# Threshold attention into a bilinear FFN: one head's keys per partition half, turned weights moved unit by unit

## The chip, the cores and the metric

The kernel runs on one core of a Trainium2 chip. The metric is the time on the device in microseconds, from the start to the end of the program. The times of one kernel on this chip differ from run to run by a few microseconds. All arithmetic is in fp32.

## The reference

Inputs: q, k, v of 8 batches x 8 heads x 576 rows x 64, a scalar tau of 0.02, and three FFN weight matrices of float64 (512 x 1536 twice, 1536 x 512).

```python
scores = scale * np.matmul(q, k.transpose(0, 1, 3, 2))
thresh = np.max(scores, axis=-1, keepdims=True) - tau
scores = np.where(scores >= thresh, scores, -1000000000.0)
scores = scores - np.max(scores, axis=-1, keepdims=True)
attn = np.exp(scores)
attn = attn / (np.sum(attn, axis=-1, keepdims=True) + 1e-09)
attn_out = np.matmul(attn, v)
# (B,H,S,D) -> (B*S, H*D)
x = attn_out.transpose(0, 2, 1, 3).reshape(B * S, H * D)
out = (x @ w_a) * (x @ w_b) @ w_out
```

So each head has a 576 x 576 matrix of weights, of which only the scores near the row's maximum are not zero; its product with v is 64 wide, and the eight heads of a row side by side are one token of 512 for the FFN.

## The kernel before

**Tiles.** Two heads make a pair; there are 32 pairs (`pairs`, four per batch). The rows of a pair are cut into five *units*: u = 0 to 3 are 128 query rows of both heads, u = 4 (`NT`) is the tail, the last 64 rows of both heads in one tile. That makes 160 units, in the order of the list `units`: for each batch first u = 0 and 1 of its four pairs, then u = 2, 3 and 4 of each pair. (Batch 0 has an order of its own: all u = 0, all u = 1, then 2 and 3 of each pair, then the four tails.)

**Slots.** The main loop runs over *slots* g. Slot g computes the scores of unit g (`scores`, matmuls at L337), takes their row maximum on VectorE (L344), the exponential on ScalarE (L372) into a tile `tw`, and the comparison with the threshold together with the row sum on VectorE (L375); the rows are divided by their sum on ScalarE (L394). Slot g+1 turns the weights of unit g, since the product with v needs the keys on the partitions. This is done in two steps: VectorE transposes blocks of 32 x 32 (`turn_blocks`, L445 and L458), and then DMAs carry the blocks to a DRAM buffer `swap` (L453, L465) and back into SBUF in the turned order (`turn_back`, L476). Two units, u = 0 and 1, or u = 2, 3 and the tail, make a *half*: `turn_blocks` writes after the second one, in four DMAs from a tile that both share; the tail adds four. One DMA brings the whole half back into `turned_sb`, of which there is one for halves. `PV_LAG` = 4 slots after the half's last unit the product with v is computed (`weighted`, `product`, L491), with v as the stationary operand and the turned weights moving. The first eight units (`BY_PE`) are turned on TensorE instead (`turn_pe`, L418 and L424), and their product follows two slots later (`weighted_unit`).

**The product.** 1152 keys of two heads lie in nine blocks of 128 partitions: blocks 0 to 3 and half of block 4 belong to head 0, the rest to head 1. A matmul reads 64 partitions (the half r) and writes 64 (the half j, one head). Each head has its keys on both halves, so each head has two sums, one per PSUM bank, and `join` adds them: a copy of the first on ScalarE (L480) and an addition of the second on VectorE (L481). Block 4 is used once by each head, on (r, j) = (0, 0) and (1, 1).

**The FFN.** When all four pairs of a half of a batch are done, their 256 tokens become a block for the FFN (`ffn`, L622, L683, L728, L774), whose matmuls are cut into small steps. `advance` works off steps between the pieces of attention, as many as a pace says: `pace` is worked out from the backlog and the slots left until the next block arrives, and the columns of products with v are set against it (`running["owed"]`).

**Order.** Each engine executes its instructions in the order in which the loop emits them (`keep_order`). SyncE (SP) issues nearly all DMAs, one queue in that order: in a slot first weights for the FFN, then `turn_blocks`' writes, then `turn_back`'s read, then loads of q, k and v, then output stores. A DMA that has to wait holds up those behind it.

**TensorE's quarters.** All large matmuls are 64 x 64: they use one quarter of the 128 x 128 array, chosen by the half of the partitions that they read and the half that they write. An fp32 matmul is recorded as two passes. Scores of a full unit use all four quarters; those of a tail have head 0's result in the upper half and head 1's in the lower, so they use (0, 1) and (1, 0) alone (`o = t if u < NT else 1 - j`).

Of the kernel before, what the change touches and what calls it, by code (L numbers as in the profile page):

```python
# [10 lines left out]
FP32 = mybir.dt.float32  # L11
# [11 lines left out]
PV_LAG = 4  # L23
# [10 lines left out]
RAWS = 4  # L34
BY_HEAD = 16
# [16 lines left out]
def kernel(  # L52
# [81 lines left out]
    def load(i, name, engine=nc.sync):  # L134
# [7 lines left out]
        for j in range(2):  # L142
            rows = src[b, 2 * hp + j].rearrange("(n e) d -> e n d", e=Q)
            for h in range(2):
                r = slice((2 * j + h) * Q, (2 * j + h + 1) * Q)
                engine.dma_start(t[r], rows[:, n0:n1, h * Q:(h + 1) * Q])
# [10 lines left out]
    def load_v(i):  # L157
        b, hp = pairs[i]
        vm = loads.tile([P, NSLOT, D], FP32, tag="vm", bufs=HP, name="vm")
        rows = v[b, 2 * hp:2 * hp + 2].rearrange("j s d -> (j s) d")  # L160
        nc.sync.dma_start(vm, rows.rearrange("(s p) d -> p s d", p=P))
        loaded[i]["v"] = vm
# [36 lines left out]
    turned_sb = const.tile([P, NSLOT * (HALF + TAIL)], FP32, name="turned_sb")  # L199
# [66 lines left out]
    t = work.tile([P, 2 * NB, 2 * Q], FP32, tag="tw", bufs=2, name="rows")  # L266
    t = t.rearrange("p n e -> p (n e)")[0:R]
    rooms = [t[:, c:c + ROWS] for c in range(0, 3 * ROWS, ROWS)]
# [29 lines left out]
    prepared, scored, weights, turned, tbufs = {}, {}, {}, {}, {}  # L298
    x_of, xtail_of = {}, {}
    blocks, complete, swaps, ready = [], [], {}, []  # L300
# [47 lines left out]
    def rooms_of(i, u):  # L348


        g = units.index((i, u))
        if u == NT and i >= HP:
            return [work.tile([P, NB, Q], FP32, tag="wt", bufs=1, name="wt")]
        if (i == 0 if u == NT else g % 2 == 0 if g < BY_PE else u % 2 == 0):
            state["tw"] = work.tile([P, 2 * NB, 2 * Q], FP32, tag="tw", bufs=2, name="tw")
        t = state["tw"]
        if u < NT and g >= BY_PE:
            return [t[:, j * NB:(j + 1) * NB, (u % 2) * Q:(u % 2 + 1) * Q] for j in range(2)]
        t = t.rearrange("p n e -> p (n e)").rearrange("p (z n e) -> p z n e", z=4, e=Q)
        return [t[:, i]] if u == NT else [t[:, g % 2 * 2 + j] for j in range(2)]  # L360
# [44 lines left out]
    def turned_at(c, n):  # L405
        return turned_sb[:, c:c + NSLOT * n].rearrange("p (s w) -> p s w", w=n)

    def turn_pe(i, u):

        ws, dg = weights.pop((i, u))  # L410
        ws = [w.rearrange("p n e -> p (n e)") for w in ws]
        wT = turned_at(units.index((i, u)) % 2 * NSLOT * P, P)
        turned[i, u, "pe"] = wT
        tp = banks(512, "tp").rearrange("p j (s q) -> p j s q", s=NT)
        for j, w in enumerate(ws):
            for s in range(NT):
                c = TAIL * j + s * P
                nc.tensor.matmul(tp[:, j, s, :], w[:, c:c + P], dg[:, j], start=True, stop=True)  # L418
        for j in range(2):
            nc.scalar.copy(wT[:, 5 * j:5 * j + NT], tp[:, j])  # L420
        tp = banks(P, "tp")[:, 0]
        for j, w in enumerate(ws):
            c = MAIN * (1 - j)
            nc.tensor.matmul(tp[TAIL * j:TAIL * (j + 1)], w[:, c:c + TAIL], dg[:, j],  # L424
                             start=True, stop=True)
        nc.vector.tensor_copy(wT[:, NT], tp)
# [10 lines left out]
    def turn_blocks(i, u):  # L437

        ws, _ = weights.pop((i, u))
        if u < NT:  # L440
            if u % 2 == 0:
                tbufs[i] = state["tw"]
            tb = tbufs[i]
            for w in ws:
                nc.vector.transpose(w, w)  # L445
            if u % 2 == 0:
                return
            h = u // 2
            n = width(i, h)
            swap = scratch.tile([2 * NB, Q, n], FP32, tag=f"swap{n}", name="swap")  # L450
            swaps[i, h] = swap
            for g in range(G):
                nc.sync.dma_start(  # L453
                    swap[:, :, g * 2 * Q:(g + 1) * 2 * Q].rearrange("c p w -> p c w"),
                    tb[g * Q:(g + 1) * Q])
        else:
            tb = ws[0]
            nc.vector.transpose(tb, tb)  # L458
            if i < HP:
                swaps[i, 2] = scratch.tile([2 * NB, Q, TAIL], FP32, tag="swapt", name="swap")  # L460
            swap = swaps[part(i, u)]
            for g in range(G):
                c = slice((1 - g // 2) * NB, (2 - g // 2) * NB)
                w0 = swap.shape[2] - TAIL + (g % 2) * Q
                nc.sync.dma_start(swap[c, :, w0:w0 + Q].rearrange("c p w -> p c w"),  # L465
                                  tb[g * Q:(g + 1) * Q])
        if part(i, u):
            ready.append(part(i, u))

    def turn_back(count):  # L470

        for _ in range(count):
            i, h = ready.pop(0)
            n = width(i, h)
            wT = turned_at((i - 1) % HP * NSLOT * TAIL if n < HALF and i else NSLOT * HALF if n < HALF else 0, n)
            nc.sync.dma_start(wT, swaps.pop((i, h)).rearrange("(s r) p w -> (r p) s w", r=G))  # L476
            turned[i, h] = wT
# [5 lines left out]
    def product(wT, vm, n):  # L483

        pv = banks(n, "pv")
        for s in (NT, 0, 1, 2, 3):
            for r in range(2):
                rows = slice(r * D, (r + 1) * D)
                for j in ((r,) if s == NT else range(2)):
                    k0 = NT if s == NT else 5 * j + s  # L490
                    nc.tensor.matmul(pv[j * D:(j + 1) * D, r], vm[rows, k0], wT[rows, k0],  # L491
                                     start=(s == (NT if j == r else 0)), stop=(s == NT - 1))
        return pv

# [24 lines left out]
    def weighted_unit(i, u):  # L519

        b, hp = pairs[i]
        pv = product(turned.pop((i, u, "pe")), loaded[i]["v"], P)
# [3 lines left out]
        join(x_of[b, 0][:, hp, u * P:(u + 1) * P], pv[:, 0], pv[:, 1])  # L526
# [6 lines left out]
    def weighted(i, h):  # L533
# [3 lines left out]
        pv = product(turned.pop((i, h)), loaded[i]["v"], n)  # L537
        if h < 2:
            if hp == 0:
                x_of[b, h] = x_tile("xT")  # L540
            lo, hi = (pv[:, r, 0:HALF].rearrange("p (i t e) -> p i t e", t=2, e=Q) for r in range(2))
            join(x_of[b, h][:, hp, :].rearrange("p (t i e) -> p i t e", t=2, e=Q), lo, hi)
            if hp == HP - 1:
                complete.append((x_of.pop((b, h)), ("half", b, h)))
        if n % HALF:
# [3 lines left out]
            join(xtail_of[b // GT][:, hp, t * TAIL:(t + 1) * TAIL], pv[:, 0, n - TAIL:n], pv[:, 1, n - TAIL:n])  # L549
# [327 lines left out]
    for g in range(len(units) + PV_LAG):  # L877
# [7 lines left out]
        back = len(ready)  # L885
# [4 lines left out]
        pace += (NSLOT + 1) // 2 * S / (NT + 1) + CATCH_UP * max(backlog() - BLOCK_COLS, 0)  # L890
        if 2 <= g < BY_PE + 2:
            weighted_unit(*units[g - 2])
            running["owed"] -= (NSLOT + 1) // 2 * P
# [51 lines left out]
        for p in range(1, NPR):  # L945
            if g == first[p] - 1:
                load_v(p)
# [53 lines left out]
```

## Time and profile before

| | |
|---|---|
| median of 3 runs | 1473.26 us (1469.57 to 1474.38) |
| the profiled execution | 1478.44 us, of which the span of its instructions is 1476.5 us |
| granted TensorE clock, mean | 0.994 |
| DMA | 626402 packets, 221.19 MB |
| products with v (L491) | 2592 passes: 1008 of 320 columns, 1152 of 256, 288 of 128, 144 of 64 |
| ScalarE copy and VectorE addition of the two sums, 256 wide | 373 and 421 ns, x60 |
| writes of full units to `swap` | 240 of 288 KB, 5.4 us from issue to landing |
| reads of halves from `swap` | 28 of 1440 KB, 7.2 us; 32 of 1152 KB, 6.2 us |

Busy shares are of the span of 1476.5 us. In lists of groups a line gives the source line, engine and operation, what is written and read, the shape and the count, then the busy time, the mean of one, and the idle time of the engine ahead of it with what ended it. In a timeline the first number is the start and the second the time from the first start to the last end of the instructions merged into the line. A pass of a matmul is recorded with its latency, so its length (377 ns for 256 columns) is longer than the distance to the next pass on the same quarter. "PEld" are weight loads, "SPq" is SP's sequencer.

### The profile page before, as it was taken

The numbers are of one execution on the slowest core, as the hardware profiler recorded it, in microseconds if no ns is written. First come the engines' busy times: TensorE is split into PE (matmuls) and PEld (weight loads), VectorE is DVE, ScalarE is ACT, GpSimd is POOL, SyncE is SP. The second block draws the span as 40 slices with busy tenths as digits, with TensorE's granted clock in tenths as the row PEclk, the third lists the DMA queues.
The fourth block names the chain that finished last, engine by engine and source line by source line (L and its number), as shares of the span: only waits on it lengthen the run. The fifth ranks groups of instructions, "written<-read, shape, count | busy, mean of one in ns | idle before, by whom it ended". The sixth has DMA issues, their size and how long they took to land.

```text
span 1476.5 us, 63772 instructions
## 1 busy us (share of the span) xinstructions
PE 1408.0 (95%) x28416; PEld 1225.4 (83%) x28416; DVE 1001.0 (68%) x2195; ACT 686.3 (46%) x1259; POOL 489.7 (33%) x678
## 2 busy tenths in 40 slices
PE   5878999989999999999999999999999999999998
PEld 4777688868988688878898988888888879899998
DVE  5998777778766876686656776677756776634324
ACT  5977455545554554554444544454544544431011
POOL 2763603233151605142425133331515060615000
PEclk9999999999999999999999999999999999999999
DMA  9966889788867886777746877578766867550000
GB/s 206 229 178 168 181 162 209 180 175 184 177 148 152 171 196 136 176 165 160 156 114 133 186 165 162 112 174 174 169 151 131 180 151 173 119 137 17 3 16 17
DMA packets 626402, 221.19 MB, mean 150 GB/s; under 512 B 544720, under 2 KB 613840, under 8 KB 626128
## 3 DMA queue, kind: packets, MB, share of 16 engines
q1 hardware_dynamic: 623760, 216.52, 67.2%
q8 instruction: 223, 3.65, 1.0%
q10 hardware_dynamic: 2368, 0.59, 0.2%
q14 instruction: 51, 0.42, 0.1%
HBM read 127.40 MB, written 89.65 MB: 147 GB/s over the span
## 4 chain that ended last, share of the span: by engine, by line
PE 84%; DVE 8%; issue 3%; ACT 2%; DMA 2%; SPq 1%; DVEq 0%; ACTq 0%
PE pab L683 32%; PE po L728 20%; PE pab L622 11%; PE pv L491 9%; PE sc L337 9%; DVE mx L344 2%; PE po L774 1%; DVE tw L445 1%; DVE tw L375 1%; DMA swap<-tw 1%; SPq L453 1%; DVE low L246 0%; ACT tw L372 0%; DVE xT L481 0%; PE tp L418 0%
## 5 line engine op out<-in xcount | busy, mean ns | idle before, releaser
L344 DVE TENSOR_REDUCE mx<-sc 128x1 f32<-128x576 f32 x288 | 205.0, 749 | 117.1 <-PE sc L337 112.5
L394 ACT ACTIVATE tw<-tw,rcp 128x576 f32<-128x576 f32 x244 | 176.1, 768 | 142.3 <-DVE rcp L388 142.3
L728 PE MATMUL po<-wo_sb,h 64*64 64x256 f32 x3264 | 227.4, 377 | 5.3 <-DVE t L640 5.3
L372 ACT ACTIVATE tw<-sc,bias,scalars 128x576 f32<-128x576 f32 x260 | 216.3, 832 | 13.0 <-issue 2.6
L337 PE MATMUL sc<-kT,qT 64*64 64x288 f32 x2016 | 208.5, 407 | 7.2 <-issue 4.2
L375 DVE SCALAR_TENSOR_TENSOR tw<-sc,thr,tw 128x576 f32<-128x576 f32 x260 | 202.6, 801 | 16.1 <-ACT tw L372 15.5
L728 PEld LDWEIGHTS po<-wo_sb,h 64*64 64x64 f32 x3264 | 167.3, 133 | 32.7 <-DVE t L640 6.2
L588 POOL TENSOR_TENSOR t<-u,t 128x512 f32<-128x512 f32 x14 | 17.8, 1272 | 532.6 <-ACT t L629 532.6
L683 PE MATMUL pab<-xS,wa_sb 64*64 64x256 f32 (+1 forms) x2560 | 187.1, 368 | 0.2 <-issue 0.2
L683 PE MATMUL pab<-xS,wb_sb 64*64 64x256 f32 (+1 forms) x2560 | 183.5, 367 | 0.0
L491 PE MATMUL pv<-turned_sb,vm 64*64 64x320 f32 (+3 forms) x2592 | 180.2, 378 | 2.7 <-DVE h L691 1.7
L697 POOL TENSOR_TENSOR h<-h 128x256 f32<-128x256 f32 x168 | 117.4, 730 | 181.1 <-PE po L728 177.5
L445 DVE STREAM_TRANSPOSE tw<-tw 128x576 f32<-128x576 f32 x240 | 171.5, 752 | 0.0
L683 PE MATMUL pab<-xT,wb_sb 64*64 64x256 f32 (+1 forms) x2304 | 166.0, 369 | 5.7 <-DVE h L691 2.6
L728 PE MATMUL po<-sums_u,h 64*64 64x256 f32 x2448 | 169.5, 379 | 0.0
L683 PE MATMUL pab<-xT,wa_sb 64*64 64x256 f32 (+1 forms) x2304 | 158.1, 365 | 5.0 <-DVE tw L375 3.2
L491 PEld LDWEIGHTS pv<-turned_sb,vm 64*64 64x64 f32 x2592 | 133.8, 132 | 27.9 <-issue 2.9
L683 PEld LDWEIGHTS pab<-xS,wa_sb 64*64 64x64 f32 x2560 | 139.8, 134 | 14.9 <-POOL xS L501 2.1
L683 PEld LDWEIGHTS pab<-xS,wb_sb 64*64 64x64 f32 x2560 | 138.9, 134 | 12.9 <-issue 0.5
L337 PEld LDWEIGHTS sc<-kT,qT 64*64 64x64 f32 x2016 | 124.5, 133 | 30.1 <-issue 10.3
L728 PEld LDWEIGHTS po<-sums_u,h 64*64 64x64 f32 x2448 | 125.9, 134 | 21.5 <-issue 0.4
L683 PEld LDWEIGHTS pab<-xT,wb_sb 64*64 64x64 f32 x2304 | 122.7, 135 | 20.4 <-DVE h L691 2.9
(127 smaller groups left out, 2119.0 us busy)
## 6 DMA issues: line engine op xcount, KB each, us to landing
swap<-tw SPq DMA_DIRECT2D x240, 288.0 KB, 5.4
turned_sb<-swap SPq DMA_DIRECT2D x28, 1440.0 KB, 7.2
turned_sb<-swap SPq DMA_DIRECT2D x32, 1152.0 KB, 6.2
vm<-in_v_dram SPq DMA_DIRECT2D x32, 288.0 KB, 5.1
kT<-in_k_dram SPq DMA_DIRECT2D x112, 72.0 KB, 5.2
swap<-wt SPq DMA_DIRECT2D x112, 72.0 KB, 2.9
out_dram<-kept SPq DMA_DIRECT2D x30, 256.0 KB, 4.8
raw<-in_moe_w_a_dram SPq DMA_DIRECT2D x18, 256.0 KB, 6.8
```

The source lines that it names most:

```text
L337: nc.tensor.matmul(sc[j if u < NT else 0][to, c], qT[r, q0:q0 + D], kT[r, c * SH:(c + 1) * SH], start=True, stop=True)
L344: nc.vector.tensor_reduce(mx[:, c], sc[j], axis=AX.XY, op=ALU.max)
L372: nc.scalar.activation(wb[j], sb[j], AF.Exp, bias=bias[:, j:j + 1], scale=e_scale)
L375: nc.vector.scalar_tensor_tensor(out=wv, in0=sb[j], scalar=thr[:, j:j + 1], in1=wv, op0=ALU.is_ge, op1=ALU.mult, accum_out=sums[:, j:j + 1])
L394: nc.scalar.activation(w, w, AF.Copy, scale=rcp[:, j:j + 1])
L445: nc.vector.transpose(w, w)
L491: nc.tensor.matmul(pv[j * D:(j + 1) * D, r], vm[rows, k0], wT[rows, k0], start=(s == (NT if j == r else 0)), stop=(s == NT - 1))
L588: (nc.vector if state["over"] else nc.gpsimd).tensor_tensor(*a, **kw)
L622: nc.tensor.matmul(pab[c * D:(c + 1) * D, r, y * P:(y + 1) * P], w[k][rows, w0:w0 + D], moving[k][rows], start=(k == 0), stop=(k == HP - 1))
L683: nc.tensor.matmul(pab[c * D:(c + 1) * D, r], w[rows, f // n, k, fs + c * D:fs + (c + 1) * D], moving, start=(k == 0), stop=(k == H - 1))
L697: (nc.vector if state["over"] else nc.gpsimd).tensor_tensor(*a, **kw)
L728: nc.tensor.matmul(po[c * D:(c + 1) * D, r, y], ht[rows, t0:t0 + D], other[rows, f], start=(f == 0), stop=(f == NF // 2 - 1))
```

## The change

The keys of head 0 lie on partitions 0 to 63 and those of head 1 on 64 to 127, in nine slots of 64 (`product`, `load_v`). A matmul therefore reads the half of its own head. The queries of a half are split instead: bank y of `pv` holds the results of the one unit or the other, and the head j writes to the partition half c = j xor y. Nothing has to be added; `settle` copies bank 0 on ScalarE, and bank 1 on VectorE in two copies that put the two halves of the partitions in each other's place. A product has 36 matmuls of n/2 columns, nine to each quarter, where there were 18 of n.

The turned weights move per unit: four writes in pieces of 9 x 32 floats, 1,152 bytes, and one read into a tile `wT` (two buffers; the group G in it takes the tail of a half, whose read is split in two). To get such pieces, the order of the keys is changed where k and v are loaded: k's row index is split as (e n) rather than (n e), and v is loaded in four DMAs to match. The first four pairs load v a second time, since their first units are turned on TensorE with the keys in order. `turn_pe` makes 18 matmuls of 64 columns wide where there were eight of 128 and two of 64. The tile `tw` holds one unit, in three buffers. `PV_LAG` is 3. The accounts of the pace count 9/2 columns for each query where they counted 5.

The scores' matmuls are the same as before, tail included.

```diff
-PV_LAG = 4
+PV_LAG = 3
+TW_BUFS = 3
...
-            rows = src[b, 2 * hp + j].rearrange("(n e) d -> e n d", e=Q)
+            rows = src[b, 2 * hp + j].rearrange("(e n) d -> e n d" if name == "k" else "(n e) d -> e n d", e=Q)
...
-    def load_v(i):
+    def load_v(i, again=False):
         b, hp = pairs[i]
-        vm = loads.tile([P, NSLOT, D], FP32, tag="vm", bufs=HP, name="vm")
-        rows = v[b, 2 * hp:2 * hp + 2].rearrange("j s d -> (j s) d")
-        nc.sync.dma_start(vm, rows.rearrange("(s p) d -> p s d", p=P))
-        loaded[i]["v"] = vm
+        if not again:
+            loaded[i]["v"] = loads.tile([P, NSLOT, D], FP32, tag="vm", bufs=HP, name="vm")
+        for j in range(2):
+            rows, half = v[b, 2 * hp + j], loaded[i]["v"][j * D:(j + 1) * D]
+            if i >= HP or again:
+                if i < HP:
+                    rows = rows.rearrange("(c s p) d -> p c s d", c=2, p=Q)
+                else:
+                    rows = rows.rearrange("(p c s) d -> p c s d", c=2, p=Q)
+                for c in range(2):
+                    nc.sync.dma_start(half[c * Q:(c + 1) * Q], rows[:, c])
+            else:
+                nc.sync.dma_start(half, rows.rearrange("(s p) d -> p s d", p=D))
...
+        for s in range(NSLOT):
+            for j, w in enumerate(ws):
+                to = (last[:, 0] if s == 2 * NT else tp[:, s // NT, s % NT])[j * D:(j + 1) * D]
+                nc.tensor.matmul(to, w[:, s * D:(s + 1) * D], dg[:, j], start=True, stop=True)
...
+        t = whole.pop((i, u))
+        for w in ws:
+            nc.vector.transpose(w, w)
         if u < NT:
...
+            swap = scratch.tile([G, P, NSLOT * Q], FP32, tag="swap", name="swap")
         else:
...
+            swap = scratch.tile([2, P, NSLOT * Q], FP32, tag="swapt", name="swap")
+        swaps[i, u] = swap
+        for g in range(G):
+            if u < NT:
+                to, n = swap[g], G
+            else:
+                to, n = swap[g % 2, (1 - g // 2) * D:(2 - g // 2) * D], 2
+            nc.sync.dma_start(to.rearrange("(r p) e -> p r e", p=Q),
+                              t[g * Q:(g + 1) * Q, 0:n * NSLOT].rearrange("p (r s) e -> p r (s e)", r=n))
+
+    def turn_back(i, u):
+
+        swap = swaps.pop((i, u)).rearrange("g p e -> p g e")
+        if u < NT or i < HP:
+            turned[i, u] = turned_tile()
+            n = G if u < NT else 2
+            nc.sync.dma_start(turned[i, u][:, 0:n].rearrange("p g s e -> p g (s e)"), swap)
+        else:
+            for y in range(2):
+                nc.sync.dma_start(turned[i, 2 + y][:, G].rearrange("p s e -> p (s e)"), swap[:, y])
...
-        pv = banks(n, "pv")
-        for s in (NT, 0, 1, 2, 3):
-            for r in range(2):
-                rows = slice(r * D, (r + 1) * D)
-                for j in ((r,) if s == NT else range(2)):
-                    k0 = NT if s == NT else 5 * j + s
-                    nc.tensor.matmul(pv[j * D:(j + 1) * D, r], vm[rows, k0], wT[rows, k0],
-                                     start=(s == (NT if j == r else 0)), stop=(s == NT - 1))
+        pv = banks(n // 2, "pv")
+        for s in range(NSLOT):
+            for j in range(2):
+                rows = slice(j * D, (j + 1) * D)
+                for c in range(2):
+                    y = j ^ c
+                    nc.tensor.matmul(pv[c * D:(c + 1) * D, y], vm[rows, s], wT[y](rows, s),
+                                     start=(s == 0), stop=(s == NSLOT - 1))
         return pv
+
+    def settle(out, pv, c0, c1):
+
+        n = c1 - c0
+        nc.scalar.copy(out[:, 0:n], pv[:, 0, c0:c1])
+        for c in range(2):
+            nc.vector.tensor_copy(out[c * D:(c + 1) * D, n:2 * n], pv[(1 - c) * D:(2 - c) * D, 1, c0:c1])
...
-            join(x_of[b, h][:, hp, :].rearrange("p (t i e) -> p i t e", t=2, e=Q), lo, hi)
+            settle(x_of[b, h][:, hp, :], pv, 0, P)
...
-        pace += (NSLOT + 1) // 2 * S / (NT + 1) + CATCH_UP * max(backlog() - BLOCK_COLS, 0)
+        pace += NSLOT * S / 2 / (NT + 1) + CATCH_UP * max(backlog() - BLOCK_COLS, 0)
...
-            turn_back(back)
+            if BY_PE + 1 < g <= len(units) + 1:
+                turn_back(*units[g - 2])
...
+        if BY_PE <= g < BY_PE + HP:
+            load_v(g - BY_PE, again=True)
```

## The prediction

> **What bounds the kernel now.** I read the page's busy shares and chain first, then the stages by window, then PE's groups by shape, then PE's timeline around the products with v, then SP's waits. The page, and the stages:
>
> ```profile
> PE 1408.0 (95%) x28416; PEld 1225.4 (83%) x28416; DVE 1001.0 (68%) x2195; ACT 686.3 (46%) x1259; POOL 489.7 (33%) x678
> PE 84%; DVE 8%; issue 3%; ACT 2%; DMA 2%; SPq 1%; DVEq 0%; ACTq 0%
> ```
>
> ```profile
> 0.00:170.00 170.00, 136.88 (x2399) 109.87 (x2400) 135.81 (x296) 115.67 (x227) 91.81 (x106) 0.98 0.87 195
> 170.00:1400.00 1230.00, 1200.48 (x24501) 1046.41 (x24498) 838.43 (x1844) 562.44 (x1018) 397.85 (x572) 1.00 0.70 152
> ```
>
> From 170 us on PE is busy 1200.5 of 1230 us, so every PE microsecond added there counts. Only the first 170 us have slack on PE (33 us idle).
>
> A busy PE here is four quarters of the array: an fp32 matmul of 64x64 is two recorded passes on the quarter given by the partition half it reads and the half it writes. Call quarters (0,0) and (1,1) diagonal, the others cross. PE's timeline around a 256-wide product, then in a run of 128-wide matmuls:
>
> ```profile
> 545.71 2.12 PE L491 MATMUL pv<-turned_sb,vm 64*64 64x256 f32 x34
> 547.49 0.41 PE L337 MATMUL sc<-kT,qT 64*64 64x288 f32 x2
> 547.65 0.40 PE L491 MATMUL pv<-turned_sb,vm 64*64 64x256 f32 x2
> 547.74 0.41 PE L337 MATMUL sc<-kT,qT 64*64 64x288 f32 x2
> 547.87 0.38 PE L622 MATMUL pab<-xT,wa_sb 64*64 64x128 f32 x2
> 547.98 0.41 PE L337 MATMUL sc<-kT,qT 64*64 64x288 f32 x2
> 547.99 0.47 PE L622 MATMUL pab<-xT,wa_sb 64*64 64x128 f32 x4
> 548.22 0.41 PE L337 MATMUL sc<-kT,qT 64*64 64x288 f32 x2
> ```
>
> ```profile
> 709.89 0.67 PE L622 MATMUL pab<-xT,wa_sb 64*64 64x128 f32 x14
> ...
> 710.33 0.67 PE L622 MATMUL pab<-xS,wa_sb 64*64 64x128 f32 x14
> ```
>
> In the second, 16 passes, four rows of four, take 710.33-709.89 = 0.44 us: 0.109 us a pass on each quarter with its weight loads hidden. In the first, 36 passes run from 545.71 to the last start near 547.67; ten passes deep on a diagonal quarter, nine intervals: 0.216 us each. The score pairs start 0.242 us apart. I take 0.27 for 320 columns and 0.136 for 160 (in proportion, estimates).
>
> The pairs of score passes that begin at 547.49, before the last pv passes start at 547.65, are the tail's: line 337 puts them on cross quarters alone. The kernel gives a product two extra matmuls on the diagonal (line 489) and the tail's four to the cross quarters, and the quarters may run past each other by about a matmul. So the lopsided product is largely paid back by the lopsided tail.
>
> **The skill.** "TensorEngine Tiling (Array Packing)", Key Properties, says that tiles work independently, weight loads included; the 0.109 us above agrees. Its Gotcha 1 says that different row tiles cannot access one PSUM bank at the same time. The new product does that (bank y takes row half y into the lower partitions and 1-y into the upper); so do the tail's scores now, and they start in pairs at 0.242 us, so for different partition halves I charge nothing. "DMA: Bandwidth & Descriptors", Specifications, asks for at least 512 B a piece; the page counts 544720 of 626402 packets below that, mostly the turned weights. The same page, Anatomy, says DMA engines wait for no semaphore, the issuing sequencer does; the trace agrees:
>
> ```profile
> SPq L476 <- DMA swap<-tw: 65.3, 29, 5.1
> SPq L476 <- PE pv L491: 39.9, 25, 4.9
> ```
>
> SP stands in these waits, and all behind it in its queue stands too.
>
> **The change part by part.**
>
> *The product.* Columns in total are unchanged: 18 matmuls of n become 36 of n/2, nine per quarter. For one pair of heads with halves of 256 and 320:
> before, diagonal: 10 x (0.216+0.27) = 4.86 us; cross: 8 x 0.486 + 4 tail passes x 0.242 = 4.86 us. They balance.
> After, every quarter: 18 x (0.109+0.136) = 4.41; cross also still has the tail, 0.97: 5.38 us. The scores are not touched, so the tail's lopsidedness now stands alone.
> If the quarters share perfectly today, the change costs 5.38-4.86 = 0.52 us a pair; if they share nothing, today costs 4.86+0.97 = 5.83 and the change saves 0.45. Over 28 such pairs: +14.6 to -12.6 us. I looked at six products' ends; in all of them other passes had started before the last pv passes. But the lead is about one matmul, and the products of u 0,1 come four in a row without a tail. I take 85% shared: before = 5.83-0.85x0.97 = 5.01, so +0.37 a pair, **+10.4 us**.
> The first four pairs: 64-column passes run at 0.058 us (36 passes of the tail's product in 0.91 us), so 18 x 0.058 = 1.04 against 10 x 0.109 = 1.09 now: nothing. Their four tail products shrink to 32 columns, not in the trace. In proportion they would take 0.029 a pass; I take the 64-column 0.058 as a floor, since loads did not shrink: 18 x 0.058 - 10 x 0.058 = 0.46, x4 = **+1.9 us** (0 at least).
> The moving operand now reads runs of 32 floats with a stride; no row shows that. Nothing if strides are free, which I take; at 10% on 4.41 us x 28 pairs it would be +12.
>
> *turn_pe, eight units.* 16 passes of 128 wide and 4 of 64 wide (2.05+0.44 us at 60 us) become 36 of 64 wide, in pairs on two column halves: 18 steps x 0.112 = 2.0 us if paired, 4.0 if not. Zero taken, +1.5 us a unit (12 us) as the upper end, and that lies in the stage with slack.
>
> *The sum of two banks.* ACT copy 373 ns, then DVE add 421 ns behind it, x60, become an ACT copy of half the width (276, the 128x128 row) and two DVE copies (271 each, from L426) that do not wait for ACT. DVE work grows by (542-421) x 60 = 7 us plus some 4 us for tails; DVE is 68% busy and PE waits some 13 us for it after 170 us. The bank comes free after about 0.55 instead of 0.8 us, and DVE no longer stands behind ACT (132.3 us idle before this add, mostly waiting for PE itself). I take **-4 us** in all, 0 to -12.
>
> *The DMAs.* Weights to turn went out as 128- and 256-byte pieces in 240+16+112 writes and came back in 64 reads; now each of 152 units has four writes and one read (two for 28 tails): 608 and 180, and v goes from 32 to 136. An issue on SP takes 0.3 to 0.6 us where the rings are not full, so 460 more cost about 200 us of SP, which has room: the 240 writes today hold SP for 316 us, 1.3 us each, because of their many pieces, and of these about a fifth remains (240 x 1152 + 128 x 576 pieces now, 120 x 512 + 32 x 256 then). DVE's transposes keep their shape. Bytes stay.
>
> *The shorter lag.* PV_LAG 3 leaves each product one slot less. The unit's read is issued behind the next unit's four writes, which wait for that unit's transposes. So the price is read from the end of the transposes of the slot before a product to the product's start, as today's positions have it: 520.92+1.43 = 522.35 to 530.38, 8.0 us, in one case; over all 63 measurable ones the median is 9.2, a tenth is under 7.6, the least 5.2. Against that: four issues of 0.5, the read's 0.4, and a landing of about 5.0 us (288 KB took 4.5 and 1152 KB took 6.2; this is 576): 7.4 us. Seven products fall short, by 5.7 us together: **+6 us** on PE, which stands in order behind them. One microsecond later makes 16.5, two make 44, one sooner 2.
>
> **Sum.** 10.4+1.9-4+6 = +14.3 us. The profiled execution's span is 1476.5 (1478.4 with what lies around it), so 1492.7 for a profile; the three timed runs have a median of 1473.3, 5 lower, so 1487.
>
> **Rivals.**
> 1. *Faster: quarters in step.* Place: the boundary behind each product. If PE's real limit makes the cross quarters wait there, a product costs five rows now and four and a half after. Price -0.45 us x 28 = -12.6 us, with the other terms at their mild ends (0 from lag and tails) 1460. It decides when less than 46% of the 0.97 us is shared (where 5.83-0.97f = 5.38). For it: the short lead, and no tail in half of a batch. Against it: the overlap at all six ends.
> 2. *No change.* Half shared, no wait on the read, some relief on DVE: +1-4+4: 1474.
> 3. *A new wait.* SP reaches the read late, or landing stays at 7 us as for today's reads: +44 in place of +6: 1525; more likely half of that, 1508. For it: four issues today took 8.04 us at 508.70. Against: a full ring of small pieces made that, and it goes.
>
> **How the numbers follow.** Forecast 0.54 (1478 to 1499), new wait 0.13, no change 0.17, quarters in step 0.16. About 0.3% (4.4 us) is what a measurement of this kernel can tell from none. Faster: 0.14 from the first rival; same: 0.14 of the second and 0.02 of the first, 0.16; slower: 0.70. The range takes half of rival 1 and half of rival 3: 1466 to 1508.
>
> **What would show it.** PE's timeline: after a tail's scores, cross quarters late by 0.97 us and nothing that pays it back. PE's waits: a group pv waiting for the DMA that writes wT, of some 6 us; 40 or more would be rival 3. PE busy should be up by about 8 us with passes of 128 columns still 0.109 apart; more would be the stride. If the span falls while PE's busy time falls by 10 us, rival 1 was right.

## The result, and the profile after

| | time | against the kernel before, on the same chip |
|---|---|---|
| kernel before | 1476.81 us (median of 12) | |
| changed kernel | 1470.76 us (median of 12, 1466.93 to 1475.83) | ratio 0.9967, 95% interval 0.9950 to 0.9984 |
| profiled execution: span | 1467.4 us, 1476.5 before | |

The forecast was 1487 us, slower. The kernel became faster by 0.33%, some 5 us by the ratio; the two profiled executions lie 9.1 us apart. The page of the changed kernel, in its busy times, the chain by engine, and the DMA packets:

```profile
PE 1404.0 (96%) x31136; PEld 1224.5 (83%) x31136; DVE 1020.5 (70%) x2295; ACT 678.8 (46%) x1259; POOL 490.4 (33%) x678
PE 81%; DVE 9%; DMA 4%; issue 2%; ACT 2%; SPq 1%; POOL 1%; DVEq 0%; ACTq 0%
DMA packets 325056, 222.82 MB, mean 152 GB/s; under 512 B 169616, under 2 KB 308880, under 8 KB 324752
```

TensorE is busy 4.0 us less than before (1408.0), and idle 63.4 us instead of 68.5. I had expected 8 us more of busy time. (The busy time itself differs a little from one profile to the next: three runs below with the same products and tails, e14 to e16, show 1403.6 to 1408.1.) VectorE has 19.5 us more work. The windows of the start and of the steady stage (busy time of PE, PEld, DVE, ACT, POOL, then clock, DMA share, GB/s):

```profile
0.00:170.00 170.00, 133.74 (x2896) 108.57 (x2900) 133.13 (x298) 112.80 (x223) 92.01 (x106) 0.98 0.88 204
170.00:1400.00 1230.00, 1208.82 (x26897) 1057.41 (x26891) 865.56 (x1953) 558.79 (x1023) 398.43 (x572) 1.00 0.61 152
```

In the steady stage TensorE idles 21.2 us where it idled 29.5; in the first 170 us it idles 3.1 us more. TensorE's waits for the turned weights, and the DMAs that carry them (count, size, median from issue to landing):

```profile
PE pv L478 <- DMA wT<-swap: 3.5, 3, 2.2
```

```profile
swap<-tw SPq DMA_DIRECT2D x480, 144.0 KB, 2.6
wT<-swap SPq DMA_DIRECT2D x120, 576.0 KB, 4.5
```

The wait that I had priced at 6 us came to 3.5, and the read lands after 4.5 us where I had taken 5.0. The product itself, on PE's timeline:

```profile
652.09 2.75 PE L478 MATMUL pv<-wT,vm 64*64 64x160 f32 x70 [0.62 <-issue]
654.56 0.40 PE L347 MATMUL sc<-kT,qT 64*64 64x288 f32 x1
654.58 0.30 PE L478 MATMUL pv<-wT,vm 64*64 64x160 f32 x2
654.68 1.17 PE L347 MATMUL sc<-kT,qT 64*64 64x288 f32 x15
```

Seventy of its 72 passes start between 652.09 and 654.58, 17.5 on each quarter: 0.142 us each with the start of the product in it. Once it runs, the trace has the passes of a quarter 0.136 us apart (653.053, 653.189, 653.325, ... 654.004), which is what I had. So the strided moving operand costs nothing that can be seen, and two row halves writing different partition halves of one bank cost nothing either. The Trainium skill, "TensorEngine Tiling (Array Packing)", Gotcha 1, warns of the latter; the run decides for this case. A tail's product of the first four pairs, with 32 columns moving:

```profile
191.04 1.23 PE L478 MATMUL pv<-wT,vm 64*64 64x32 f32 x72
```

Eighteen passes on each quarter, less the 0.22 us of latency of the last: (1.23 - 0.22) / 17 = 0.06 us a pass, the floor that I had taken.

What did not come is the relief on VectorE. The groups of the settling copies, after (busy, mean ns of one, idle ahead):

```profile
L487 DVE COPY xT<-pv 64x128 f32<-64x128 f32 (+1 forms) x136 | 38.1, 280 | 129.2 <-ACT xT L485 127.8
L485 ACT COPY xT<-pv 128x128 f32<-128x128 f32 (+1 forms) x68 | 17.7, 260 | 183.5 <-PE pv L478 183.4
```

Before, VectorE's wait ahead of the addition was

```profile
DVE xT L481 <- ACT xT L480: 132.3, 59, 6.4
```

VectorE's two copies write columns that ScalarE's copy doesn't touch and read the other bank, yet they wait for it just as the addition did: in the trace VectorE starts about 0.03 us after ScalarE's copy has ended. Most of the 127.8 us is the wait for the product itself. Only some 0.38 us of each wait lie behind the product's last pass, 22 us in all (26 before). From the start of ScalarE's copy to the end of the last one of VectorE's 0.89 us pass, where copy and addition took 0.83 before.

### The profile page after: what moved, and what is told of

Its sections match the earlier page's. It is cut to its first block, busy times and chain, and to the rows that moved or that the text cites. A ratio compares the mean times of both kernels' runs of the same rounds, so it can differ in the third digit from the quotient of the medians.

```text
span 1467.4 us, 70219 instructions
## 1 busy us (share of the span) xinstructions
PE 1404.0 (96%) x31136; PEld 1224.5 (83%) x31136; DVE 1020.5 (70%) x2295; ACT 678.8 (46%) x1259; POOL 490.4 (33%) x678
## 3 DMA queue, kind: packets, MB, share of 16 engines
q1 hardware_dynamic: 322384, 217.73, 60.1%
## 4 chain that ended last, share of the span: by engine, by line
PE 81%; DVE 9%; DMA 4%; issue 2%; ACT 2%; SPq 1%; POOL 1%; DVEq 0%; ACTq 0%
PE pab L683 33%; PE po L728 18%; PE pab L622 11%; PE pv L478 9%; PE sc L347 9%; DVE mx L354 2%; DMA wT<-swap 2%; DVE tw L441 1%; DVE tw L378 1%; SPq L452 1%; PE po L774 1%; DVE low L255 1%; DVE xT L487 0%; POOL h L697 0%; POOL xU L502 0%
## 5 line engine op out<-in xcount | busy, mean ns | idle before, releaser
L397 ACT ACTIVATE tw<-tw,rcp 128x576 f32<-128x576 f32 x272 | 197.8, 769 | 221.9 <-DVE rcp L391 221.9
L375 ACT ACTIVATE tw<-sc,bias,scalars 128x576 f32<-128x576 f32 x288 | 239.7, 832 | 9.9 <-ACT bias L374 0.2
L378 DVE SCALAR_TENSOR_TENSOR tw<-sc,thr,tw 128x576 f32<-128x576 f32 x288 | 224.2, 800 | 14.1 <-ACT tw L375 13.0
L441 DVE STREAM_TRANSPOSE tw<-tw 128x576 f32<-128x576 f32 x272 | 196.0, 754 | 0.8 <-ACT tw L397 0.8
L347 PE MATMUL sc<-kT,qT 64*64 64x288 f32 x2016 | 188.1, 404 | 2.4 <-DVE tw L378 1.5
L478 PE MATMUL pv<-wT,vm 64*64 64x160 f32 (+3 forms) x5184 | 183.6, 273 | 6.4 <-DMA wT<-swap 3.5
L478 PEld LDWEIGHTS pv<-wT,vm 64*64 64x64 f32 x5184 | 164.7, 134 | 17.0 <-issue 7.3
L728 PE MATMUL po<-sums_u,h 64*64 64x256 f32 x2448 | 158.5, 376 | 0.6 <-DVE h L645 0.6
L347 PEld LDWEIGHTS sc<-kT,qT 64*64 64x64 f32 x2016 | 111.2, 133 | 28.7 <-issue 6.3
L683 PEld LDWEIGHTS pab<-xT,wa_sb 64*64 64x64 f32 x2304 | 114.8, 134 | 22.1 <-ACT wo_sb L242 2.0
```

The lines of the kernel that those rows point to most:

```text
L347: nc.tensor.matmul(sc[j if u < NT else 0][to, c], qT[r, q0:q0 + D], kT[r, c * SH:(c + 1) * SH], start=True, stop=True)
L375: nc.scalar.activation(wb[j], sb[j], AF.Exp, bias=bias[:, j:j + 1], scale=e_scale)
L378: nc.vector.scalar_tensor_tensor(out=wv, in0=sb[j], scalar=thr[:, j:j + 1], in1=wv, op0=ALU.is_ge, op1=ALU.mult, accum_out=sums[:, j:j + 1])
L397: nc.scalar.activation(w, w, AF.Copy, scale=rcp[:, j:j + 1])
L478: nc.tensor.matmul(pv[c * D:(c + 1) * D, y], vm[rows, s], wT[y](rows, s), start=(s == 0), stop=(s == NSLOT - 1))
L683: nc.tensor.matmul(pab[c * D:(c + 1) * D, r], w[rows, f // n, k, fs + c * D:fs + (c + 1) * D], moving, start=(k == 0), stop=(k == H - 1))
```

## The experiments

Every run has a ratio to the kernel before, measured beside it. It is not the quotient of two medians, and differs a little from it. Differences between two kernels are taken from these ratios, times 1476.8 us. The interval of one ratio is 1.4 to 3.8 us to either side (5.2 in e3), so that of a difference is 3 to 5 us. e1 to e4, e5 to e8 and e9 to e16 were measured on three different chips.

| run | built on | median us | ratio, 95% interval |
|---|---|---|---|
| e1 | after | 1469.70 | 0.9952 (0.9937 to 0.9967) |
| e2 | before | 1487.08 | 1.0069 (1.0052 to 1.0085) |
| e3 | before | 1500.37 | 1.0133 (1.0098 to 1.0168) |
| e4 | before | 1473.62 | 0.9982 (0.9972 to 0.9991) |
| e5 | after | 1461.23 | 0.9890 (0.9867 to 0.9913) |
| e6 | before | 1475.94 | 0.9997 (0.9984 to 1.0009) |
| e7 | before | 1466.60 | 0.9924 (0.9904 to 0.9943) |
| e8 | after | 1473.56 | 0.9987 (0.9973 to 1.0001) |
| e9 | after | 1494.48 | 1.0111 (1.0091 to 1.0131) |
| e10 | after | 1472.87 | 0.9966 (0.9952 to 0.9980) |
| e11, lag 6 | after | 1492.13 | 1.0115 (1.0089 to 1.0141) |
| e12, lag 5 | after | 1489.59 | 1.0076 (1.0051 to 1.0102) |
| e13, lag 4 | after | 1485.68 | 1.0059 (1.0035 to 1.0083) |
| e14 | after | 1465.70 | 0.9928 (0.9906 to 0.9950) |
| e15 | after | 1474.39 | 0.9988 (0.9977 to 0.9999) |
| e16 | after | 1475.08 | 0.9980 (0.9965 to 0.9995) |

### The quarters: e2, e6, e5, e1, e8

How much of the lopsided product does the lopsided tail pay back in the kernel before? e2 puts the tail's scores on the diagonal, where the product has its two extra matmuls, so that nothing can be paid back.

```diff
-            o = t if u < NT else 1 - j
+            o = t if u < NT else j
...
```

A second hunk makes the writes to `swap` follow.

> The kernel before, with all tails' scores on the diagonal quarters, where the lopsided product is too: diagonal quarters get 1348 us of streaming, cross quarters 1317, the same surplus of 31 us as in the changed kernel, with the product and everything else as before. Theory of the quarters: 10 to 16 us slower than before. Rival (hidden): within 3 us of before. If it is slower while the changed kernel with alternating tails gains nothing, the surplus costs only where products are of long passes.

Measured: +10.2 us. A pair of heads now costs 4.86 + 0.97 = 5.83 us in my sum, against 5.83 - 0.97f before, f being the share that is paid back; 28 pairs make 27f us, so f = 0.38 (0.28 to 0.46 by the interval).

e6 spreads the kernel before's tail over all four quarters; a row of the tail then takes half of its columns from each head, so its maxima and sums are those of a mixture.

```diff
-            o = t if u < NT else 1 - j
+            o = t if u < NT else j ^ c
```

> The kernel before with the tail's score matmuls on four quarters in the same way (rows of the tail mix two heads). The lopsided product then has nothing that pays it back. If tail and product shared nearly all their surplus before (the forecast's 85%): 0.97 x 0.85 = 0.82 us of sharing goes and 0.48 us of tail goes, +0.34 us on 32 tails, 11 us slower. If they shared a third, as the slowing by 10.8 us of the run with tails on the diagonal says (of 31 us): 0.97 x 0.35 - 0.48 = -0.14 us each, 4 us faster. If they shared nothing: 15 us faster.

Measured: -0.4 us (-2.4 to +1.3). With the tail even, a pair costs 4.86 + 0.485 = 5.345 us whatever is shared; nothing changes where 5.83 - 0.97f is the same, f = 0.50 (0.41 to 0.55). At 85% it would have been +9.5 us. Two runs, two edits: 0.4 to 0.5, not 0.85. Both figures rest on the sum, in which a microsecond on the fullest quarter is one of the end.

e5 is the edit of e6 in the changed kernel (with the same mixture in the tail's rows).

> The changed kernel, with the tail's four score matmuls on four quarters (the first half of the keys of a head is put to one half of the partitions and the second to the other, so rows of the tail mix two heads; all operations and sizes are the same). Theory of quarters in step (quarters can run past each other by so little that a lopsided group is paid nearly in full, and alternating pairs could therefore gain nothing): each of 32 tails takes two rows of passes and not four, 0.48 us less, so 12 to 15 us faster than the changed kernel, about 1457. Rival (the surplus is hidden in waits for other engines): within 3 us of the changed kernel.

Measured: 0.9890 against 0.9967, -11.4 us (4 to either side), of the 13.6 that 28 even tails would give if nothing paid for the uneven ones. TensorE's busy time falls by 11.6 us (1392.4 for 1404.0). So in the changed kernel the tail does stand alone, or nearly so, as the prediction had it.

Two ways to bring that back without mixing rows failed. e1 puts the tail of every second pair on the diagonal:

```diff
-            o = t if u < NT else 1 - j
+            o = t if u < NT else (j if i % 2 else 1 - j)
...
```

> The changed kernel, with the tail's scores on the diagonal quarters for every second pair and on the cross quarters for the others, so that all four quarters have the same work (cross 1346 to about 1331 us of streaming, diagonal 1315 to 1331). Theory of the quarters (the fullest quarter sets the time, as the forecast had it): 8 to 15 us faster than the changed kernel, about 1458 against 1471. Rival (the cross quarters' surplus of 31 us over the diagonal ones is hidden in waits, or paid back at them): within 3 us of the changed kernel.

Measured: -2 us, inside the uncertainty, where even quarters gave 11. Two tails three slots apart, some 20 us, hardly pay each other. e8 computes the tails of two pairs together, one on each diagonal:

```diff
...
+                both = [(multiply(i, u), i), (multiply(i + 1, u), i + 1)]
+                for step in range(4):
+                    if step % 2 == 0:
+                        for (sc, each), _ in both:
+                            for one in each[step:step + 2]:
+                                one()
...
```

> The changed kernel, with the tails of two pairs in neighbouring slots (the second pair's tail ahead of its units 2 and 3), the second one's scores on the diagonal quarters and emitted together with the first one's, so that the eight matmuls fill all quarters evenly; nothing is left out. Theory of quarters in step: as the run with four quarters, on 28 of 32 tails, 10 to 13 us faster than the changed kernel, about 1459, if the new order costs nothing elsewhere. Rival (hidden in waits): 1468 to 1474.

Measured: +3 us against the changed kernel; a miss. The second tail has to go ahead of its pair's units 2 and 3, so either the new order costs what the even quarters give, or they give nothing in this form; I haven't separated the two. TensorE's busy time falls by 1.9 us (to 1402.1), where e5's fell by 11.6.

### Pieces and lag: e3, e4, e7

e3 is the shorter lag alone.

```diff
-PV_LAG = 4
+PV_LAG = 3
```

> The kernel before with the product three slots after the half's last unit, one constant changed. If the shorter lag is what made the changed kernel faster (blocks for the FFN arrive a slot earlier): 4 to 8 us faster than before. If the lag gives nothing and only takes slack from the read of the turned weights: slower, by 10 us or more, with waits of the products for the DMA that writes turned_sb, since writes there take 5.4 us and reads 6 to 7 us. In between (no change) neither matters.

Measured: +20 us by the ratio. TensorE's wait for the turned weights in e3 (the profile is of its longest execution, 1513.9 us, so it shows a bad case):

```profile
PE pv L491 <- DMA turned_sb<-swap: 28.4, 12, 5.6
```

e4 is longer pieces alone: the kernel before writes its blocks to `swap` in rows that follow each other there. The read then brings keys in an order that no longer matches v.

```diff
-                nc.sync.dma_start(
-                    swap[:, :, g * 2 * Q:(g + 1) * 2 * Q].rearrange("c p w -> p c w"),
-                    tb[g * Q:(g + 1) * Q])
+                n0 = 4 * NB * Q
+                to = swap.rearrange("c p w -> (c p w)")[g * Q * n0:(g + 1) * Q * n0]
+                nc.sync.dma_start(to.rearrange("(p c w) -> p c w", p=Q, w=2 * Q), tb[g * Q:(g + 1) * Q])
...
```

A second hunk does the same for the tails.

> The kernel before with the same bytes written to the DRAM buffer in contiguous rows and not in pieces of 128 and 256 bytes; the order of the keys in the buffer is therefore another, so the weights meet other rows of v. Reads, lag, product and tails are as before. Theory of the DMAs (fewer packets free SP and the rings, and PE's waits shrink): packets fall from 626 to about 300 thousand and the time by 5 to 10 us, to or below the changed kernel's. Rival (the DMAs are hidden anyway): packets fall as much and the time stays within 3 us of before.

Measured: -2.7 us (-4.1 to -1.3). The page of e4 counts

```profile
DMA packets 287970, 221.19 MB, mean 150 GB/s; under 512 B 194512, under 2 KB 263632, under 8 KB 280016
```

where there were 626402. So over half of the packets can go, and the kernel gains two or three microseconds: nearly all of the DMAs' time was hidden.

e7 is e4 and `PV_LAG` 3 (the same mismatch of keys and v).

> The kernel before with contiguous writes (another order of keys in the buffer, so weights meet other rows of v) and the product three slots after the half's last unit. If it was the short pieces that made the shorter lag cost 24 us: most of that is gone, within 8 us of the run with contiguous writes alone (1474). If it is the single buffer and the large read of a whole half: still over 1490, with waits of products for turned_sb.

Measured: -11.2 us against the kernel before and -8.6 against e4. The page of e7, TensorE's wait for the turned weights, and the writes:

```profile
PE 1403.0 (96%) x28416; PEld 1232.1 (84%) x28416; DVE 998.9 (68%) x2195; ACT 685.8 (47%) x1259; POOL 490.2 (34%) x678
```

```profile
PE pv L491 <- DMA turned_sb<-swap: 2.3, 3, 1.3
```

```profile
swap<-tw SPq DMA_DIRECT2D x240, 288.0 KB, 4.3
```

Of its span of 1463.1 us TensorE idles 60.1, where the kernel before idled 68.5; its wait for the turned weights is 2.3 us. The same edit of one number costs 20 us with short pieces and gains 8.6 with long ones. The prediction did price the lag with the faster transfers, but only as a wait; that the lag itself could give something, once they were fast enough, had no number. Where e7 gains on e4 can be read from the steady stage of both, e4 first:

```profile
170.00:1400.00 1230.00, 1201.93 (x24597) 1063.80 (x24592) 843.48 (x1854) 562.51 (x1018) 397.93 (x572) 1.00 0.60 152
170.00:1400.00 1230.00, 1206.82 (x24693) 1061.53 (x24689) 844.28 (x1863) 563.51 (x1020) 396.34 (x570) 1.00 0.61 151
```

TensorE idles 23.2 us there in e7, 28.1 in e4, and its busy time over the whole program is 3.4 us less (1403.0 for 1406.4). In the first 170 us the two idle alike (31.1 and 31.4).

### What the lag is worth: e9, e13, e12, e11

e9 gives the changed kernel its lag of 4 back and issues each read one slot later, so that the distance from read to product stays.

```diff
-PV_LAG = 3
+PV_LAG = 4
...
-            if BY_PE + 1 < g <= len(units) + 1:
-                turn_back(*units[g - 2])
+            if BY_PE + 2 < g <= len(units) + 2:
+                turn_back(*units[g - 3])
```

> The changed kernel with PV_LAG 4 again and each read of turned weights issued one slot later (three slots after its unit), so that the distance from read to product is as in the changed kernel and only the slot of the product, and with it the slot in which a block reaches the FFN, is later. Theory A (the shorter lag gains by giving TensorE its FFN work a slot sooner, above all between 90 and 160 us; 7 us in the kernel before with long pieces): 1478 us, about 7 slower than the changed kernel, most of it lost before 170 us. Theory B (the lag's gain there came with the old reads of halves and has no worth in the changed kernel): 1471, within 2 us of it.

Measured: +21 us, far more than either theory. Two side effects were suspected: three DRAM buffers no longer leave one free, and the load of v for the fifth pair stands in SP's queue ahead of the read that its buffer waits for. e13 takes both away:

```diff
-    scratch = pool("scratch", 3, space=bass.MemoryType.DRAM)
+    scratch = pool("scratch", 8, space=bass.MemoryType.DRAM)
...
-            if g == first[p] - 1:
+            if g == first[p] - 1 + (PV_LAG - 3) * (p >= HP):
```

> e9 with eight DRAM buffers for turned weights instead of three and the load of v from the fifth pair on one slot later, so that no write and no load stands in SP's queue for a read or a product that is not out yet. Theory C (e9's 24 us came from such waits in SP's queue): back to within 3 us of the changed kernel, 1473. Theories A and B: unchanged, about 1492.

e12 and e11 are e13 with lags of 5 and 6.

> As e13 with PV_LAG 5: the product of a second half now falls in the slot of a unit 3, and its last read in that of a unit 2. Theory A (each slot of lag costs, since the FFN gets its block later): 20 more than e9, about 1515. Theory B (what counts is which slot of the cycle of three has the product and its last read; with lag 4 the read falls in the tail's slot, which is short): no read in a short slot, about 1475 to 1482.

> As e13 with PV_LAG 6: the product of a second half falls in a tail's slot again, as with PV_LAG 3, but three slots later. Theory A (length of the lag): 60 more than the changed kernel, about 1530. Theory B (place in the cycle): 1472, within 4 us of the changed kernel. Between, at 1485, both would have a part.

Measured, against the changed kernel: lag 4 +13.6, 5 +16.1, 6 +21.9 us. So the two side effects together were 7.7 us of e9's loss (5 to either side); TensorE's wait for the reads falls from 12.0 to 7.5 us. The rest fits neither pure theory: lag 6 has the products in the same slots of the cycle as lag 3 and is not back (place falls), and three slots cost nowhere near 60 (my figure for length falls). The windows of e11:

```profile
0.00:170.00 170.00, 128.71 (x2746) 105.33 (x2746) 135.95 (x304) 113.98 (x225) 90.91 (x104) 0.95 0.86 198
170.00:1400.00 1230.00, 1200.40 (x26570) 1055.32 (x26574) 852.46 (x1925) 555.58 (x1018) 396.02 (x570) 1.00 0.62 153
```

In the first 170 us TensorE is busy 5.0 us less than in the changed kernel, and in the steady stage it idles 29.6 us for 21.2. The first agrees with blocks that reach the FFN later while there is nothing else to fill TensorE; no run shows that this is the cause. The second holds in both kernels: from 170 to 1400 us TensorE idles 28.1 to 36.9 us with a lag of 4 to 6 (before, e4, e9, e11 to e13), and 17.6 to 25.4 with a lag of 3 (after, e7, e10, e14 to e16). Why stays open. The wait for the reads is not the reason: it is 7.9 us in e11, but 7.8 and 7.7 in e15 and e16, with a lag of 3.

### The start stage, and VectorE: e10, e14, e15, e16

The changed kernel stays 6.4 us behind e7 (0.9967 against 0.9924). e10 turns the first eight units as before, with the old product and sum for them.

```diff
...
-                nc.tensor.matmul(to, w[:, s * D:(s + 1) * D], dg[:, j], start=True, stop=True)
+                nc.tensor.matmul(tp[:, j, s, :], w[:, c:c + P], dg[:, j], start=True, stop=True)
...
-        pv = product([lambda rows, s, t=t: t[rows, s] for t in wT], loaded[i]["v"], P)
+        pv = product_first(wT, loaded[i]["v"], P)
...
```

> The changed kernel with the first eight units as in the kernel before: eight turning matmuls of 128 columns and two of 64, v first loaded in one DMA in the old order, their product with nine blocks and the sum of two banks. Theory A (the start stage, which I had put down at nothing, costs the changed kernel about 6 us, read at equal streamed work near 90 us): 1465 us, and the difference to the changed kernel is there by 100 us and stays. Theory B (that deficit is made up later by FFN work that is waiting anyway): 1470, within 2 us of the changed kernel.

Measured: no difference (0.9966). The zero that I had put down for `turn_pe` holds. The deficit that I had read near 90 us is there and is made up later: TensorE idles 32.0 us in the first 170 of e10 (36.3 in the changed kernel), but 25.4 in the steady stage (21.2).

e14 leaves all of `settle` to ScalarE, e15 to VectorE (e14's edit first, then e15's):

```diff
-            nc.vector.tensor_copy(out[c * D:(c + 1) * D, n:2 * n], pv[(1 - c) * D:(2 - c) * D, 1, c0:c1])
+            nc.scalar.copy(out[c * D:(c + 1) * D, n:2 * n], pv[(1 - c) * D:(2 - c) * D, 1, c0:c1])
```

```diff
-        nc.scalar.copy(out[:, 0:n], pv[:, 0, c0:c1])
+        nc.vector.tensor_copy(out[:, 0:n], pv[:, 0, c0:c1])
```

> The changed kernel with all three copies of settle on ScalarE, so that VectorE neither makes its two copies (50 us in all) nor stands for ScalarE ahead of them (128 us). Theory A (the 6 us by which the changed kernel stays behind e7 are VectorE's: more copies that wait as before): 1465 to 1467. Theory B (VectorE's part costs nothing, PE seldom waits for it): 1471, within 2 us of the changed kernel; ScalarE frees the bank after about 0.27 + 2 x 0.25 us as now, so no loss either.

> The changed kernel with all three copies of settle on VectorE: the handover from ScalarE goes, VectorE gets some 18 us more work. Theory A (the handover is what costs): 1465 to 1467. Theory A' (VectorE's load is what costs): 1473 or more. Theory B: 1471, within 2 us.

Measured: e14 -5.8 us against the changed kernel, e15 +3.1. The page of e14, and of e15:

```profile
PE 1403.6 (96%) x31136; PEld 1231.8 (84%) x31136; DVE 975.6 (67%) x2095; ACT 727.7 (50%) x1459; POOL 491.4 (34%) x678
```

```profile
PE 1407.4 (96%) x31136; PEld 1237.1 (84%) x31136; DVE 1047.3 (71%) x2395; ACT 655.8 (45%) x1159; POOL 490.3 (33%) x678
```

e15 has no handover between the two engines at all and isn't faster; it is slower by an amount just clear of its interval (3.0). VectorE still waits there for the product:

```profile
DVE xT L485 <- PE pv L478: 116.9, 58, 7.1
```

So the handover is not what costs. Taking 44.9 us of work from VectorE gave 5.8 (4 to either side), adding 26.8 cost 3.1; between e14 and e15, measured side by side and both without a handover, 71.7 us of work make 8.9 us. That is about 0.12 us of the end for one of VectorE's. But e14 takes away something else too: VectorE, which works in order, no longer stands for the product. How much is load and how much is this stand the runs don't separate. VectorE's largest waits in the changed kernel and, below, in e14:

```profile
DVE xT L487 <- ACT xT L485: 127.8, 58, 6.3
DVE mx L354 <- PE sc L347: 104.5, 72, 3.8
DVE h L691 <- PE pab L683: 59.4, 15, 6.2
```

```profile
DVE mx L354 <- PE sc L347: 255.3, 126, 5.6
DVE h L691 <- PE pab L683: 61.6, 18, 6.2
```

The stand ahead of the copies has become a stand ahead of the scores: VectorE is now ready before the scores are, and starts on their row maxima at once. e14 changes no part of the computation and is faster than both kernels: 1465.70 us, 0.9928 (0.9906 to 0.9950).

e16 gives the turned weights three buffers.

```diff
-        return work.tile([P, G + 1, NSLOT, Q], FP32, tag="wT", bufs=2, name="wT")
+        return work.tile([P, G + 1, NSLOT, Q], FP32, tag="wT", bufs=3, name="wT")
```

> The changed kernel with three buffers for the turned weights instead of two, so that the first read of a half need not wait in SP's queue for the last product (102 us of SP's waits). Theory A (these waits hold up the writes and loads behind them and cost PE 3 us or more): 1467 or less. Theory B (SP has room, PE's wait for the reads is 3.5 us in all and belongs to the second read): 1470, within 2 us of the changed kernel.

Measured: 0.9980, no gain. SP's standing for the last product in the changed kernel,

```profile
SPq L461 <- PE pv L478: 102.5, 45, 4.7
```

is gone in e16; SP stands for the transposes instead (410.3 us for 330.0). It cost nothing that can be seen.

## Why the prediction was wrong

Its sum was +14.3 us; the measured change is -4.9. From the kernel before to e4, e7 and the changed kernel the ratios give:

| step | forecast | measured |
|---|---|---|
| pieces alone (e4) | 0 | -2.7 |
| shorter lag, with these pieces (e7 against e4; the +6 was for reads by unit) | +6 | -8.6 |
| new product, its copies, reads by unit, new start (after against e7) | 10.4 + 1.9 - 4 = +8.3 | +6.4 |

**The step that failed is the shorter lag.** "PV_LAG 3 leaves each product one slot less" was only read as a loss; that a block reaches the FFN, and the buffers come free, a slot sooner was given no number. In place of +6 us the runs show -8.6 (e7 against e4, 3 to either side), and longer lags in the changed kernel cost 13.6 to 21.9. The loss itself was well sized: TensorE waits 3.5 us for the reads in the profile of the changed kernel, 5.9 to 7.8 in those of e10 and e14 to e16, for 6. With TensorE idle 33 us in the first 170 and 29.5 after, there was room for a gain, and I had shown that room myself. The gain of e7 came in the steady stage, where TensorE's idle time fell from 28.1 to 23.2 us, and in a shorter busy time. Which of the things that start sooner brings it isn't shown.

**"I take 85% shared"** failed too. e2 and e6 say 38 and 50%. With these, the term of the quarters is 28 x (5.38 - 5.83 + 0.97f) = -2.3 to +1.0 us instead of +10.4. With the ends of their intervals it is -5 to +2. That passes of the next work start before the last passes of a product shows that the quarters can run ahead, not that they do so by the whole difference. Nor does the tail stand beside the product as a rule: in the trace of the kernel before 24 of the 28 tails begin 5.9 to 10.7 us after the last pass of a product, with other work between. The first rival's decision point, 46%, lies within what was measured.

**Two DVE copies "that do not wait for ACT"** failed: they do wait for it, 58 times, and the bank comes free after 0.89 us, not 0.55. Nothing shows the -4. Instead the added 19.5 us of work on VectorE cost some 19.5 x 0.12 = 2.3 us, an estimate from e14 and e15; I had foreseen 11 us of it and charged nothing, with VectorE 68% busy.

The third row of the table came out near its forecast by luck: two of its terms were wrong in opposite directions. With quarters at -2.3 to +1.0, the narrow tails at +1.9 and VectorE at +2.3, 1.9 to 5.2 of the 6.4 us are accounted for; the rest is within the uncertainty of the difference.

**Right** were: strides free; nothing for a shared bank; the start stage at nothing (e10); 32-column passes with a floor of 0.058 us; SP has room for the many small DMAs (e16): a write to `swap`, in fewer pieces now, holds SP 0.5 us on the mean, where it held it 1.3. That full rings made the 1.3 us isn't shown.

**"What would show it"**: the tail in the changed kernel is paid nearly in full (e5), the wait for wT is of the size named; busy time up by 8 us was wrong, it fell by 4, or stayed the same within what profiles differ.

**The rivals.** By the ratio the result is 1468 on the scale of the three runs that I forecast from, between the second rival (1474) and the first (1460). It came by neither's way: half shared and little wait was in the second, relief on VectorE, also in the second, didn't come, and the gain from the lag was in none. The third rival, a new wait, didn't come with long pieces; with short ones it is e3. My figure for half of it was summed wrongly: 22 us in place of 6 make 1503, not 1508.

## What to carry to other kernels

Price two edits of a change together where one makes the other possible: a lag that is shortened because its transfers got faster has a gain to be priced, in what may start sooner, beside the wait that it risks. An overlap that is seen at some ends isn't a share; an edit that takes it away altogether, and one that makes it needless, bracket it in two runs. Load on an engine that isn't the busiest need not be free when it stands between two pieces of work of the busiest one (here 0.12 us for one, at 70% busy): move it to the idler engine and measure.

## What the runs showed of the hardware

- Taking away over half of the DMA packets (626402 to 287970, the bytes unchanged) gave 2.7 us of 1477 where the transfers were hidden. The Trainium skill, "DMA: Bandwidth & Descriptors", Specifications, asks for 512 B a piece; here longer pieces (still 194512 packets under 512 B) were worth a faster landing (a write of 288 KB 4.6 us for 5.4) and a shorter lag, and little by themselves.
- Quarters of the array make up for each other only in part: a surplus of 0.97 us on one pair of quarters was recovered to about 40 to 50% (28 to 55% by the intervals of e2 and e6, an estimate from the sum) by work of the same size on the other pair, mostly 6 to 11 us later; of two such surpluses some 20 us apart (e1) hardly anything was.
- A pass of 64x64 with 32 columns moving takes 0.06 us on its quarter ((1.23 - 0.22) / 17, from a product of 72 passes with 0.22 us of latency), as much as one with 64 in the kernel before (0.058).
- Copies of VectorE into other columns of a tile, from another bank, waited for ScalarE's copy into the same tile: they started about 0.03 us after its end in 58 waits. Taking this handover away altogether (e15) gained nothing.
